# Moving a kernel's one odd-sized step from the last place to the last but one

## The chip, the cores and the metric

One core of one Trainium2 chip. The metric is device time in microseconds for one execution; a profiled run also gives the span from the first to the last instruction, some 2 us less.

In the profile's lines PE is TensorE (matmuls), PEld its loads of weights, DVE VectorE, ACT ScalarE, POOL GpSimd, which here also issues loads, and L443 is a line of the kernel. A line of a timeline has start and duration in us, engine, line, operation, output <- inputs, how many are merged (x4), and in brackets how long the engine stood idle before it and what ended that.

## The reference

The input x is 8 batches of 4224 tokens with 192 channels; t and s below index tokens.

```
x  = causal 7-tap convolution of the input, softmax taps per head (8 heads of 24 channels)
th = x @ w_theta
y  = w_tok_r @ (x * cos(th)) + w_tok_i @ (x * sin(th))       # over the 4224 tokens
u  = x + y
out = u + relu(u @ w_ch)
```

Nearly all the work is the two 4224 x 4224 token matmuls over 8 x 192 = 1536 columns.

## The kernel before

4224 tokens are 33 **row blocks** of 128 output tokens and 33 **chunks** of 128 input tokens. A chunk is prepared (convolution, transposes, theta, sine, products, sums) into seven fp16 operands `z`; up to 11 chunks are held at a time. A **step** visits a unit of row blocks with the active chunks. Sixteen units are pairs, done with seven products per chunk; unit 16 is the **single** block 32, with four. Each chunk meets all 17 units in 17 consecutive steps.

```python
    NU = (NT + 1) // 2                      # 17 units, NT = 33 row blocks
    ...
    base = [0, 0, 1, 1, 2, 3, 3, 4, 4, 5, 5]
    ...
    start = [base[k % NW] + (NU + 1) * (k // NW) for k in range(NK)]
    NSTEP = start[-1] + NU                  # 58
    shift = (NU - 1 - (NSTEP - 1)) % NU     # the single in step 57 (and 6, 23, 40)
    ...
    def unit(t):
        return (t + shift) % NU
```

Partial sums go to device memory between visits. x has to be added to each row block once. Where it can, GpSimd adds it to a block while it is loaded ("adds"); for the last five steps, which are short, an accumulating transfer adds it to the stored partial block beforehand ("ahead"), at a step worked out from the step's number:

```python
        self.late = self.final and self.n < NW
        ...
                if not self.late:
                    self.adds.append(i)
                else:
                    far = known <= start[2 * NW - 1]
                    self.ahead.append((i, 2 * NU - NW + 2 * (t % NU) if far else start[-1],
                                       (t // NU - 1 - far) % 2))
```

Work that is not a token matmul is placed among those of a step by position, in sevenths of the step. The positions that matter here:

```python
        for j, (r, i, which) in enumerate(here):        # additions "ahead"
            found.append((1.5 + 1.8 * j, lambda ...: r.add_ahead(i, which)))
        ...
            found.append((1.3 + 3 * (m - 1), lambda m=m: nxt.load_w(m)))    # weights for t + 2
        ...
                found.append((4.5, lambda k=k: load_chunk(k)))    # x of chunks that start at t + 2
        ...
                pos = [0, .5, 1.4, 2.2, 2.6, 3.1, 3.15, 3.4, 3.6]   # preparing a chunk for t + 1
```

The weights' loads and the additions are pinned in order on GpSimd's queue; the loads of x (`xw`, four per chunk) are not, and the framework's scheduler places them.

Of the kernel before, what the change touches and what calls it, by code (L numbers as in the profile page):

```python
# [16 lines left out]
def kernel(  # L17
# [42 lines left out]
    NU = (NT + 1) // 2  # L60
# [4 lines left out]
    assert len(base) == NW  # L65
    start = [base[k % NW] + (NU + 1) * (k // NW) for k in range(NK)]
    NSTEP = start[-1] + NU
    shift = (NU - 1 - (NSTEP - 1)) % NU

    NOSYNC = mybir.DependencyInfo(  # L70
        mybir.DependencyClass.NoSync, mybir.DependencyReason.DATA
# [664 lines left out]
```

## Time and profile before

Median 1449.51 us in the runs that the prediction had. The prediction shows the lines of the profile and what its steps take (y: token matmuls). Beside these, steps 0 to 3, which prepare the first chunks, take 86 us.

To read the steps: a step's y is known from the code, at 0.325 us per run of two matmuls (an unbroken stretch of the trace before has 104 in 16.90 us). What a step lasts beyond its y is the other work of TensorE plus its waits, and a comparison of such excesses, step by step, finds a lost microsecond in 58 steps.

### The profile page before, as it was taken

Reading aid. Unit: us, or ns where it says so; the run is one execution under the profiler, and the core shown is the slowest. Engines: PE = TensorE matmul, PEld = TensorE weight load, DVE = VectorE, ACT = ScalarE, POOL = GpSimd, SP = SyncE. Lnnn points to the kernel's source line nnn. Section 1 sums busy time; section 2 is a strip of 40 time slices with the busy share of each in tenths; the row PEclk is TensorE's granted clock in tenths of the full one; section 3 lists DMA queues with packets and bytes.
Section 4 is the critical chain, followed back from the end, with each engine's and each line's share of the span. In section 5 each row is a group of like instructions: output and inputs, shape, how many; then the busy total and the mean of one; then the engine's idle time right before and its main releaser. Section 6 shows DMA issues by size and latency. Waiting matters only on the chain.

```text
span 1446.4 us, 23748 instructions
## 1 busy us (share of the span) xinstructions
PE 1416.3 (98%) x9809; PEld 887.9 (61%) x9809; DVE 979.2 (68%) x1051; ACT 315.5 (22%) x379; POOL 435.1 (30%) x655
## 2 busy tenths in 40 slices
PE   7899999999999999999999999999999999999997
PEld 5556666666666666666666666666666666666665
DVE  6893555545548777866666657877777667767686
ACT  5861101111134254000000004435210110010133
POOL 7431211111233232432433342233323123213120
PEclk9999999999999999999999999999999999999999
DMA  9986756465699998998899989999999999998893
GB/s 173 227 178 145 146 103 149 90 149 97 137 231 219 214 250 217 228 254 183 213 256 213 242 143 245 228 188 234 279 216 206 209 204 221 204 203 194 166 222 125
DMA packets 272029, 281.99 MB, mean 195 GB/s; under 512 B 106672, under 2 KB 240176, under 8 KB 271920
## 3 DMA queue, kind: packets, MB, share of 16 engines
q0 software_dynamic: 162464, 92.15, 48.4%
q1 hardware_dynamic: 71824, 178.88, 35.1%
q10 hardware_dynamic: 37632, 9.44, 4.1%
q8 instruction: 77, 1.26, 0.3%
q14 instruction: 32, 0.26, 0.1%
HBM read 245.49 MB, written 108.13 MB: 244 GB/s over the span
## 4 chain that ended last, share of the span: by engine, by line
PE 89%; DVE 4%; DMA 3%; POOL 2%; ACT 1%; issue 1%; SPq 0%; DVEq 0%; ACTq 0%; POOLq 0%
PE y L443 82%; PE v L141 5%; PE pc L210 1%; PE tp L165 1%; POOL st L323 1%; DMA xw<-in_x_dram 1%; DVE z L257 1%; DVE wt L336 1%; DVE pv L408 1%; ACT z L246 1%; DVE z L251 0%; DVE pv L476 0%; DVE wt L348 0%; POOL xw L197 0%; DMA xs<-z 0%
## 5 line engine op out<-in xcount | busy, mean ns | idle before, releaser
L443 PE MATMUL y<-z,wt 128*128 128x384 f16 x7656 | 1283.6, 326 | 10.6 <-DVE pv L408 7.5
L443 PEld LDWEIGHTS <-wt 128*128 128x128 f16 x7656 | 740.8, 98 | 488.6 <-issue 10.6
L408 DVE TENSOR_TENSOR pv<-y,pv 128x768 f32<-128x768 f32 x324 | 308.9, 954 | 323.6 <-PE y L443 282.8
L336 DVE STREAM_TRANSPOSE wt<-st 128x1408 f16<-128x1408 f16 (+7 forms) x224 | 327.8, 1465 | 48.5 <-PE y L443 39.0
L323 POOL DMA_DIRECT2D st<-in_moe_w_tok_r_dram x232 | 132.5, 578 | 466.1 <-DVE wt L336 461.0
L323 POOL DMA_DIRECT2D st<-in_moe_w_tok_i_dram x232 | 132.7, 578 | 404.4 <-DVE wt L336 388.9
L348 DVE TENSOR_TENSOR wt<-wt 128x1408 f16<-128x1408 f16 (+7 forms) x216 | 176.7, 818 | 40.8 <-PE y L443 38.4
L151 ACT ACTIVATE z<-pc 128x768 f16<-128x768 f32 x65 | 53.2, 819 | 387.2 <-PE pc L210 386.9
L151 ACT ACTIVATE ub<-pv 128x768 f16<-128x768 f32 x63 | 50.2, 835 | 333.0 <-DVE pv L408 310.4
L406 ACT ACTIVATE pv<-y 128x768 f32<-128x768 f32 x66 | 54.0, 819 | 282.0 <-PE y L443 282.0
L141 PEld LDWEIGHTS <-uT 128*128 128x128 f16 x1056 | 91.0, 98 | 25.8 <-issue 7.9
L386 POOL TENSOR_TENSOR pv<-pv,xr 128x1536 f32<-128x1536 f32 x24 | 74.5, 3105 | 68.6 <-DVE pv L476 22.1
L197 POOL DMA_DIRECT2D xw<-in_x_dram x132 | 76.4, 585 | 31.0 <-DMA xw<-xw 8.7
L476 DVE SCALAR_TENSOR_TENSOR pv<-v,pv 128x768 f32<-128x768 f32 x66 | 62.9, 954 | 27.5 <-PE v L141 27.1
L257 DVE TENSOR_TENSOR z<-z 128x768 f16<-128x768 f16 x132 | 73.4, 556 | 3.6
L151 ACT ACTIVATE uT<-tp 128x1536 f16<-128x1536 f16 (+1 forms) x48 | 58.2, 1215 | 74.4 <-PE tp L165 74.4
L246 ACT ACTIVATE z<-v,half_pi 128x768 f16<-128x768 f32 x66 | 59.8, 907 | 41.2 <-PE v L141 40.8
L251 DVE TENSOR_TENSOR z<-z 128x1536 f16<-128x1536 f16 x66 | 60.0, 947 | 7.5 <-ACT z L246 7.5
L141 PE MATMUL v<-wth,uT 128*128 128x192 f16 x528 | 55.0, 248 | 4.4 <-ACT z L246 3.0
L141 PE MATMUL v<-wch,uT 128*128 128x192 f16 x528 | 54.2, 246 | 2.1 <-DVE pv L476 1.2
L246 ACT ACTIVATE z<-v 128x768 f16<-128x768 f32 x66 | 53.4, 809 | 0.0
L210 PE MATMUL pc<-xw,bands 96*64 96x192 f16 x528 | 35.8, 258 | 2.6 <-ACT bands L625 1.1
(44 smaller groups left out, 142.4 us busy)
## 6 DMA issues: line engine op xcount, KB each, us to landing
part<-pv SPq DMA_DIRECT2D x79, 768.0 KB, 4.3
pv<-part SPq DMA_DIRECT2D x79, 768.0 KB, 6.1
out_dram<-pv SPq DMA_DIRECT2D x66, 384.0 KB, 4.3
st<-in_moe_w_tok_r_dram POOLq DMA_DIRECT2D x136, 176.0 KB, 5.5
st<-in_moe_w_tok_i_dram POOLq DMA_DIRECT2D x136, 176.0 KB, 5.1
xs<-z SPq DMA_DIRECT2D x132, 96.0 KB, 4.5
xw<-in_x_dram POOLq DMA_DIRECT2D x121, 96.0 KB, 6.1
xr<-xs SPq DMA_DIRECT2D x24, 384.0 KB, 3.7
```

What stands on the lines that cost most here:

```text
L141: pe(nc.tensor.matmul(v[:, k, b * D : (b + 1) * D], lhsT=tT[:, 3 * k + b + i, :], rhs=w[:, 2 * b + i, :], start=(i == 0), stop=(i == 1),))
L151: act(nc.scalar.activation(out=out, in_=in_, func=AT.Copy))
L197: nc.gpsimd.dma_start(out=self.xw[lo : lo + n, h, :, :], in_=x[:, t0 : t0 + n, :].rearrange("b s d -> s b d"),)
L246: act(nc.scalar.activation(**args))
L257: dve(nc.vector.tensor_tensor(out=z[:, o, :], in0=z[:, a, :], in1=z[:, b, :], op=ALU.subtract))
L323: pool(nc.gpsimd.dma_start(out=st[a * Q : (a + 1) * Q, 0:nb, :, 0:n] .rearrange("i r bt s -> i (r bt) s"), in_=w[self.tbs[0] * P : (self.t ...
L336: dve(nc.vector.transpose(self.w[name][:, 0 : self.n, :, :], self.st[int(name[1])][:, int(name[0]) - 1, :, 0 : self.n * Q] .rearrange("p b ...
L348: dve(nc.vector.tensor_tensor(out=self.w[name][:, 0 : self.n, :, :], in0=self.w[a][:, 0 : self.n, :, :], in1=self.w[b][:, 0 : self.n, :, : ...
L386: ins = pool(nc.gpsimd.tensor_tensor(out=self.pv[i], in0=self.pv[i], in1=self.xr[i], op=ALU.add))
L408: dve(nc.vector.tensor_tensor(out=o, in0=yv, in1=o, op=ALU.add))
L443: pe(nc.tensor.matmul(y[cn][:, q, 0:BH], lhsT=self.w[wn][:, c, :, :].rearrange("p bt i -> p (bt i)"), rhs=chunks[k].z[:, zn, q * BH : (q + ...
L476: dve(nc.vector.scalar_tensor_tensor(out=ub, in0=channel_mix(self.uT[i][:, 6 * g : 6 * g + 6, :], wch), scalar=0.0, in1=ub, op0=ALU.max, o ...
```

## The change

Its intent is a better end: the single, the cheapest visit, is taken one step earlier, and the last step, when only two chunks are left, is a pair. One constant rotates the whole order of units.

```diff
-    shift = (NU - 1 - (NSTEP - 1)) % NU
+    shift = (NU - 1 - (NSTEP - 2)) % NU
```

The single moves from steps 6, 23, 40, 57 to 5, 22, 39, 56; all units, and the row blocks with them, move one step earlier.

## The prediction

> **What bounds the kernel now.** I read the page's engine table first, then the chain of waits, then cut TensorE's timeline into the kernel's 58 steps.
>
> ```profile
> PE 1416.3 (98%) x9809; PEld 887.9 (61%) x9809; DVE 979.2 (68%) x1051; ACT 315.5 (22%) x379; POOL 435.1 (30%) x655
> ...
> PE 89%; DVE 4%; DMA 3%; POOL 2%; ACT 1%; issue 1%; SPq 0%; DVEq 0%; ACTq 0%; POOLq 0%
> PE y L443 82%; PE v L141 5%; PE pc L210 1%; PE tp L165 1%; POOL st L323 1%; DMA xw<-in_x_dram 1%; DVE z L257 1%; DVE wt L336 1%; DVE pv L408 1%; ACT z L246 1%; DVE z L251 0%; DVE pv L476 0%; DVE wt L348 0%; POOL xw L197 0%; DMA xs<-z 0%
> ...
> L443 PE MATMUL y<-z,wt 128*128 128x384 f16 x7656 | 1283.6, 326 | 10.6 <-DVE pv L408 7.5
> ```
>
> The reader is to see that TensorE is busy 98% of the span and that token-mixing matmuls (y) alone carry 82% of the chain. Their 326 ns mean is an overlapped duration: 7656 of them lie in 1283.6 us of busy time, and the chain's unbroken stretches have 104 in 16.90 us, 0.1625 us each. One run of a weight against a chunk is two of them, 0.325 us.
>
> The code gives the length of every step: a pair of row blocks costs 7 runs per active chunk, the single block 4. Counting y matmuls along TensorE's timeline places each step. In most steps the time is y plus the other matmuls, with no gap: a pair with 11 chunks takes 25.0 us (y 25.04), one that also prepares two chunks and has 9 takes 26.7 (y 20.49, 6.2 of preparation). Two places differ: the single step that also prepares two new chunks (step 40), and the tail. The windows of steps 39, 40, 56, 57 and of what follows the last y matmul:
>
> ```profile
> core 0: us, PE busy (x) PEld busy (x) DVE busy (x) ACT busy (x) POOL busy (x), PEclk, DMA share, GB/s
> 975.20:1001.90 26.70, 26.70 (x216) 17.20 (x214) 17.46 (x23) 12.33 (x14) 9.17 (x16) 1.00 1.12 228
> 1001.90:1021.50 19.60, 18.51 (x163) 11.70 (x161) 17.43 (x20) 12.22 (x14) 4.04 (x8) 1.00 0.98 296
> 1412.40:1427.00 14.60, 13.74 (x114) 9.36 (x112) 10.34 (x13) 6.21 (x8) 0.00 (x0) 1.00 0.26 83
> 1427.00:1431.40 4.40, 4.12 (x32) 2.50 (x30) 3.93 (x6) 1.54 (x2) 0.00 (x0) 1.00 0.26 89
> 1431.40:1446.40 15.00, 6.89 (x78) 5.42 (x75) 7.31 (x9) 5.41 (x7) 0.00 (x0) 0.96 0.47 159
> ```
>
> Step 39 has TensorE full; step 40, 7 us shorter, does not. The last 15 us have every engine under half busy. There a cycle of cast, transpose, evacuation, channel matmul and final add runs, as the timeline's last lines show:
>
> ```profile
> 1430.77 1.82 DVE L408 TENSOR_TENSOR pv<-y,pv 128x768 f32<-128x768 f32 x2 [0.43 <-PE y L443]
> ...
> 1438.32 0.96 DVE L476 SCALAR_TENSOR_TENSOR pv<-v,pv 128x768 f32<-128x768 f32 x1 [0.98 <-PE v L141]
> 1438.60 0.34 PEld L165 LDWEIGHTS <-ub 128*128 128x128 f16 x6 [0.62 <-ACT ub L151]
> ...
> 1439.15 0.81 ACT L151 ACTIVATE uT<-tp 128x768 f16<-128x768 f16 x1 [0.60 <-PE tp L165]
> ...
> 1440.19 1.82 DVE L476 SCALAR_TENSOR_TENSOR pv<-v,pv 128x768 f32<-128x768 f32 x2 [0.91 <-PE v L141]
> ```
>
> VectorE adds the last token-mix sums at 1432.6 and finishes the last output at 1442.0, 9.4 us later; 4.4 us more go to the last store and the end.
>
> [...]
>
> **The change, part by part.** One constant rotates the order of the row blocks. Nothing is removed. Each chunk still meets all 17 units once, so y stays at 7656 matmuls, and counting from the code gives the same 79 partial stores, 79 loads, 24 additions of x and 9 early additions. The single moves from steps 6, 23, 40, 57 to 5, 22, 39, 56.
>
> *Start, steps 5 to 7: 0.* The four start-up steps with gaps (extras of 15.9, 14.2, 11.4 and 3.9 us over y) come before step 5 and keep their chunks. The single with 11 chunks took 14.30 us, all y, and will do so one step earlier.
>
> *Middle.* Before, of three inner singles only step 40 prepares two chunks while it runs. After, step 22 and step 39 both do, each with 9 chunks; step 40 becomes an ordinary pair. Step 40 took 19.58 us: y 11.71, so 7.87 of other time against 6.19 in step 39. Being squeezed costs 7.87 - 6.19 = **1.7 us**. Two squeezes in place of one: **+1.7**. Step 41 also loses 0.5 to what VectorE is left with (25.50 against 25.04); this too occurs about twice in place of once, **+0.4**.
>
> *Last steps.* Before: step 56, pair with 4 chunks, 28 runs; step 57, single with 2, 8 runs. After: single with 4, 16 runs; pair with 2, 14 runs. Six runs leave the end, 6 x 0.325 = 1.95 us; these lie in earlier steps, where TensorE is full, so step 56 begins **+1.95** later. What follows must be shorter by that to break even.
>
> From the start of step 56 to the last token add, the trace has 1412.4 to 1432.6 = **20.2 us**. After, VectorE limits this stretch. In step 56 TensorE has 5.2 us of y and about 4 of the previous step's transposes and outputs; VectorE has leftovers of step 55 (1.8), 3 additions of 0.95, 3 outputs of 0.96, and the next pair's weights: 4 transposes of 0.43 and 4 sums of about 0.25 (estimated from 0.41 for twice the size). That is about 10.3 us. In step 57 y is 14 x 0.325 = 4.55 us but there are 7 additions. Back to back each takes 0.91 (1.82 for two), so 6.4; with one more output 0.96 and a cast 0.55, about 7.9. TensorE must wait for each addition before it writes the same of its two sum buffers again. The sum is **18.2 us**, 2.0 less than before.
>
> After the last addition: still six output halves, but now two row blocks complete together. I walked the order of the code with the trace's durations (cast 0.55 or 0.84, transposes 0.5, evacuation 0.81, channel matmuls 0.82, final add 0.96, 0.1 for a hand-over). The two halves of the single are ready at once; the four of the pair share ScalarE (four evacuations, two casts: 4.9 us) and the two buffers of transposes and channel results. The last final add ends at about **10.0 us**, against 9.4 before: **+0.6**. Store and end: 4.4 in both.
>
> Sum: 1.7 + 0.4 + 1.95 - 2.0 + 0.6 = **+2.65 us**. To this I add 0.6 for the chance of the transfer wait below.
>
> **Rivals.** (1) *A transfer wait in step 39.* Its 26.7 us become about 19.6, while it loads x for the last two chunks, weights for two steps on and two partial blocks in place of one. The DMA share was already 1.12 there. The code lets the chunks' loads start in the middle of the step, and their median landing in this stretch is 8.0 us. Had they to wait, TensorE's first convolution of step 40 would stop for 2 to 6 us: 1455 to 1458. Against it: step 40 before moved 296 GB/s at a share of 0.98 with little loss. I give it one in five. (2) *A shorter tail.* If the outputs after the end overlap better than my walk, or step 57's additions hide beside TensorE, the last stretch gains 3 to 4 us and the total is a tie, 1448 to 1450. For it: VectorE has more work before the end in the new order and so less is left idle. Against it: two blocks end at once and only one engine evacuates. (3) *VectorE bounds the last steps harder.* If the seven additions alternate with TensorE rather than overlap, each round costs 0.95 + 0.65 + 0.1 for some of them, adding 2 to 3 us: 1455.
>
> **Range and chances.** 1449.5 + 2.65 + 0.6 = **1452.8 us**. The terms are uncertain by some 2 us each at the tail and up to 6 in step 39, so **1449.0 to 1457.0**. Two per cent is 29 us, the whole length of the tail; no term comes near. Faster by over 2%: 0.005; within: 0.985; slower: 0.01. The direction is less sure than the verdict: slower than before at about 85%.
>
> **What would show it.** y matmuls 7656 as before. Steps 22 and 39 about 19.6 us with 1 to 2 us of gaps, step 40 about 26.7 (longer with a wait of the convolution for x: rival 1). Step 56 starting 3.5 to 4.5 us later than 1412.4. VectorE nearly unbroken through steps 56 and 57, TensorE's y waiting on additions there. The last final add about 10 us after the last addition. The prediction is wrong if a transfer stalls TensorE in steps 22 to 24 or 38 to 41, or the tail changes by more than 3 us.

That a run keeps its price in another step, on which the +1.95 rests, was the assumption; in the result the 7656 y matmuls took 1283.2 us against 1283.6.

## The result, and the profile after

The changed kernel took **1457.72 us** (median of 4, 1454.78 to 1458.70) against 1449.14 (1448.48 to 1449.61). The ratio is 1.0056, 95% interval 1.0039 to 1.0074: slower by 0.6%, and within 2%. It was outside the predicted range by 0.7 us. (A ratio is the mean time of one kernel's runs over that of the other's of the same rounds, so not quite the ratio of the medians.)

The profiled run was the fastest of the four: span 1452.7 us against 1446.4. Its page's engine table, the head of its chain of waits, and the convolution's group:

```profile
PE 1415.5 (97%) x9809; PEld 886.8 (61%) x9809; DVE 976.8 (67%) x1051; ACT 315.2 (22%) x379; POOL 434.3 (30%) x655
...
PE 86%; DMA 6%; DVE 5%; ACT 2%; issue 1%; POOL 1%; SPq 0%; DVEq 0%; POOLq 0%; ACTq 0%
...
L210 PE MATMUL pc<-xw,bands 96*64 96x192 f16 x528 | 35.5, 255 | 6.0 <-DMA xw<-in_x_dram 3.7
```

TensorE's work is the same (1415.5 against 1416.3 us), but DMA's share of the chain rose from 3% to 6%, and the convolution now waits for the load of x, a releaser that its row of before did not name.

Excess over y by step, in the two profiled runs (of steps 0 to 55, those not listed agree within 0.2 us; 56 and 57 are taken together with the end, below):

| step | before: runs, excess | after: runs, excess |
|---|---|---|
| 22 | 63, 6.19 | 36 (single), **7.86** |
| 23 | 44 (single), 0.00 | 77, 0.46 |
| 36 | 63, 6.26 | 63, **9.02** |
| 39 | 63, 6.19 | 36 (single), **7.86** |
| 40 | 36 (single), 7.87 | 63, 6.59 |
| 41 | 77, 0.46 | 77, 0.00 |

Step 56 starts at 1413.63 us before and at 1420.31 after: 6.68 later. Six runs of y that now lie earlier are 1.95 of it, steps 22, 23, 39, 40 and 41 together 2.04, and **step 36 alone 2.76**. From there to the end it is 32.77 before and 32.39 after.

Step 36 is neither a single nor beside one. Windows of steps 35 and 36, first the kernel before, then after (columns as in the prediction's windows):

```profile
868.40:895.00 26.60, 26.60 (x215) 17.18 (x214) 20.57 (x25) 12.33 (x14) 9.12 (x16) 1.00 0.95 219
895.00:921.80 26.80, 26.80 (x217) 17.27 (x215) 22.46 (x28) 12.33 (x14) 6.87 (x12) 1.00 1.04 235
```

```profile
873.00:899.70 26.70, 26.70 (x216) 17.21 (x214) 21.27 (x26) 12.32 (x14) 11.59 (x19) 1.00 1.06 256
899.70:929.20 29.50, 26.98 (x216) 17.31 (x214) 22.38 (x28) 12.32 (x14) 7.87 (x14) 1.00 1.10 249
```

TensorE is idle for 2.5 us of step 36 after, and in step 35 GpSimd issues 19 instructions in place of 16. The timeline of GpSimd's issues and of the convolution shows which. Before:

```profile
875.80 2.29 POOL L323 DMA_DIRECT2D st<-in_moe_w_tok_r_dram  x4 [12.48 <-DVE wt L336]
878.08 2.29 POOL L197 DMA_DIRECT2D xw<-in_x_dram  x4
...
890.38 2.29 POOL L323 DMA_DIRECT2D st<-in_moe_w_tok_i_dram  x4 [10.02 <-DVE wt L336]
892.65 2.29 POOL L197 DMA_DIRECT2D xw<-in_x_dram  x4
```

After:

```profile
879.80 2.28 POOL L323 DMA_DIRECT2D st<-in_moe_w_tok_r_dram  x4 [12.49 <-DVE wt L336]
882.07 3.46 POOL L395 DMA_DIRECT2D part<-xs  x4
...
886.94 1.22 POOL L197 DMA_DIRECT2D xw<-in_x_dram  x2 [1.42 <-DMA st<-in_moe_w_tok_r_dram]
...
894.38 2.27 POOL L323 DMA_DIRECT2D st<-in_moe_w_tok_i_dram  x4 [6.21 <-DVE wt L336]
...
896.64 2.27 POOL L197 DMA_DIRECT2D xw<-in_x_dram  x4
...
902.91 0.52 PE L210 MATMUL pc<-xw,bands 96*64 96x192 f16 x7 [2.52 <-DMA xw<-in_x_dram]
```

Before, the four loads of the first chunk leave directly after the weights. After, four accumulating transfers (`part<-xs`, 384 KB each) stand there; they landed 10.0 us after their issue (median), where two stores of 768 KB in the same step took 5.1. Only two of the chunk's loads follow them, 13.9 us into the step (886.9 less its start at 873.0) where before's four left at 9.1 (878.1 less 869.0); the other two come behind the second weights (`st<-in_moe_w_tok_i_dram`), whose issue waits for VectorE to free a buffer (6.21 us). They leave at 896.6 and 897.2, and step 36 wants them at 900.1. They land 6.0 and 5.7 us after their issue, sooner than the 8.1 to 8.7 us that the four took before: they came late because they left late, not because they moved slowly.

Why they are there: the step of an early addition is 2 x 17 - 11 + 2 x (t mod 17). For the last step, t = 57, it is 35. Before, the last step was block 32, whose tokens come too late for that and are added in step 41; the others came out as 27, 29, 31 and 41. With blocks 0 and 1 last, the formula applies and gives 35, in which two chunks are prepared and two are loaded. The number of early additions, nine, is unchanged; their place is not.

### The profile page after: what moved, and what is told of

The parts are those of the page before. It is cut to its first block, busy times and chain, and to the rows that moved or that the text cites. A ratio compares the mean times of both kernels' runs of the same rounds, so it can differ in the third digit from the quotient of the medians.

```text
span 1452.7 us, 23747 instructions
## 1 busy us (share of the span) xinstructions
PE 1415.5 (97%) x9809; PEld 886.8 (61%) x9809; DVE 976.8 (67%) x1051; ACT 315.2 (22%) x379; POOL 434.3 (30%) x655
## 4 chain that ended last, share of the span: by engine, by line
PE 86%; DMA 6%; DVE 5%; ACT 2%; issue 1%; POOL 1%; SPq 0%; DVEq 0%; POOLq 0%; ACTq 0%
PE y L443 78%; PE v L141 5%; DMA st<-in_moe_w_tok_r_dram 1%; DMA xw<-in_x_dram 1%; PE pc L210 1%; PE tp L165 1%; DVE pv L408 1%; DMA xs<-z 1%; DVE wt L336 1%; ACT z L246 1%; DMA xw<-xw 1%; DVE z L257 1%; DVE z L251 1%; POOL st L323 1%; DMA pv<-part 1%
## 5 line engine op out<-in xcount | busy, mean ns | idle before, releaser
L443 PE MATMUL y<-z,wt 128*128 128x384 f16 x7656 | 1283.2, 326 | 12.8 <-DVE pv L408 9.7
L348 DVE TENSOR_TENSOR wt<-wt 128x1408 f16<-128x1408 f16 (+7 forms) x216 | 173.4, 803 | 43.4 <-PE y L443 41.1
```

The costliest lines, as they stand in the source:

```text
L348: dve(nc.vector.tensor_tensor(out=self.w[name][:, 0 : self.n, :, :], in0=self.w[a][:, 0 : self.n, :, :], in1=self.w[b][:, 0 : self.n, :, : ...
L443: pe(nc.tensor.matmul(y[cn][:, q, 0:BH], lhsT=self.w[wn][:, c, :, :].rearrange("p bt i -> p (bt i)"), rhs=chunks[k].z[:, zn, q * BH : (q + ...
```

## The experiments

**Theory.** The change costs what the prediction said of squeezed singles and of the end, and beyond that a wait for x in step 36 that comes from where the additions of blocks 0 and 1 are issued. **Rival one:** the wait belongs to the position of the single. **Rival two:** it is the additions' bytes, not their place in the queue. Four kernels ran first, on one chip, 5 rounds, with the kernel before at a median of 1449.91 us (1446.70 to 1453.93, 11 runs).

**r1, the changed kernel again.**

> The changed kernel once more, beside the others on the same chip. In its first profile step 36 lost 2.8 us to a convolution waiting for x, yet the profiled run (1454.8 us) was the fastest of four (up to 1458.7), so some 3.5 us more vary from run to run. Theory: the wait in step 36 is longer in other runs, expected median 1455 to 1459 with a spread of 2 to 4 us. Rival: the spread is chance of the chip that day, then before's runs here spread as much.

Median 1457.34 us (1456.72 to 1459.32), ratio 1.0057. As expected. Its spread is not beyond that of before in these rounds, so the rival about the spread is not excluded; but its profiled run, 1457.37 us, shows what a slower execution does. Step 36 lost 5.92 us (12.18 over y against 6.26). Windows around its wait (the last three columns: granted clock, DMA share, GB/s):

```profile
899.00:902.00 3.00, 0.81 (x5) 0.26 (x3) 2.97 (x4) 0.00 (x0) 2.27 (x4) 0.96 1.43 198
902.00:906.00 4.00, 3.19 (x15) 1.69 (x16) 0.14 (x1) 0.81 (x1) 0.00 (x0) 0.50 1.18 371
906.00:910.00 4.00, 4.00 (x24) 1.97 (x22) 0.71 (x1) 0.81 (x1) 0.00 (x0) 0.68 1.07 301
```

TensorE waited 3.00 us, and then its clock was 0.50 and 0.68 for 8 us: the wait was paid about twice. In the first profile a wait of 2.52 us left the clock at 1.00 (over the next 8 us). Step 3 shows the same of one fixed wait. TensorE stands 2.46 us there in all eleven profiles. In five of them (before, after, r1, r5, r7) its clock is 1.00 over the next 3 us and the step has 3.94 us over y; in the other six it is 0.54 to 0.64 and the step has 5.62. So two profiles can differ by 1.7 us in a step that no edit touches, and it is safer to compare steps than spans. The length of the wait alone does not decide what the clock does next: it was lower after 1.98 us (r7: 0.63 over 4 us), 2.46 (step 3, six profiles) and 3.00 (r1), and 1.00 after 2.46 (step 3, five profiles), 2.52 (the first profile) and 3.53 (r4 below, over 898 to 906 us). What does decide it is not shown.

**r2, the additions in a quiet step.**

```diff
-                    self.ahead.append((i, 2 * NU - NW + 2 * (t % NU) if far else start[-1],
+                    self.ahead.append((i, min(2 * NU - NW + 2 * (t % NU), 33) if far else start[-1],
```

> The changed kernel with one edit: the early additions of x to row blocks 0 and 1 are issued in step 33 (a quiet step) in place of step 35 (which prepares two chunks and loads two more). Theory: these four accumulating transfers stand ahead of the chunk loads and are the cause of the 2.8 us wait in step 36, so steps 35 and 36 go back to 26.7 us each, the time is 1449.1 + 3.5 = 1452 to 1453 us, and the spread falls to below 1 us. Rival: the wait comes from the rotation itself (other weights and rows at that time), then step 36 keeps over 1.5 us of gap and the time stays at 1455 to 1458.

1453.48 us (1452.74 to 1454.48), ratio 1.0026; 0.5 above the expected band and with a spread of 1.7 us, not below 1. Step 36 is back to 6.26 over y, and GpSimd's queue has the order of before in steps 35 and 36:

```profile
881.75 2.28 POOL L323 DMA_DIRECT2D st<-in_moe_w_tok_r_dram  x4 [12.49 <-DVE wt L336]
884.01 2.28 POOL L197 DMA_DIRECT2D xw<-in_x_dram  x4
896.33 2.28 POOL L323 DMA_DIRECT2D st<-in_moe_w_tok_i_dram  x4 [10.03 <-DVE wt L336]
898.60 2.28 POOL L197 DMA_DIRECT2D xw<-in_x_dram  x4
```

So the additions' place costs 1457.34 - 1453.48 = 3.9 us in the medians. Steps 22, 23, 39, 40 keep 7.86, 0.47, 7.86, 6.59.

**r3, the position of the single without the move of blocks 0 and 1.**

```diff
-            self.tbs = [tb for tb in (2 * self.u, 2 * self.u + 1) if tb < NT]
+            v = self.u if self.u == NU - 1 else (self.u - 1) % (NU - 1)
+            self.tbs = [tb for tb in (2 * v, 2 * v + 1) if tb < NT]
```

> The changed kernel with the same positions of pair and single, but the row blocks renamed so that the last pair is blocks 30 and 31 as in the kernel before (step 56 the single, step 57 the pair 30, 31) and no early addition falls into step 35. Theory: only the squeezes (+1.7, +0.4) and the shift of 6 runs with the shorter tail (+1.95 - 0.4) remain: 1452 to 1453.5 us, step 36 without a gap. Rival (the position of the single causes the wait in step 36): 1455 to 1458 us.

1453.91 us (1451.21 to 1454.01), ratio 1.0024; the median is 0.4 above the band. Step 36: 6.25 over y, no gap. The single stands where the change put it, and the wait is gone: rival one falls. What is left, about 4 us over before, is the position's own cost.

**r4, the suspected cause put into the kernel before.**

```diff
-                    self.ahead.append((i, 2 * NU - NW + 2 * (t % NU) if far else start[-1],
+                    self.ahead.append((i, (35 if t == 55 else 2 * NU - NW + 2 * (t % NU)) if far else start[-1],
```

> The kernel before with one edit: the early additions of row blocks 28 and 29 are issued in step 35 in place of step 31. Theory: the suspected cause alone, put into the kernel before, brings its wait: step 36 gets 2 to 4 us of gap behind a load of x, the time is 1451.5 to 1458 us and spreads more. Rival: nothing happens (within 0.7 us of before), and the wait in the changed kernel needs the new rotation.

1455.35 us (1454.36 to 1456.92), ratio 1.0040. Step 36: 10.05 over y, and the convolution waits as in the changed kernel:

```profile
898.46 0.27 PE L210 MATMUL pc<-xw,bands 96*64 96x192 f16 x1
902.26 0.52 PE L210 MATMUL pc<-xw,bands 96*64 96x192 f16 x7 [3.53 <-DMA xw<-in_x_dram]
```

The cause alone, with every unit in its old place, brings the wait. Gap and time are as expected; the spread, 2.6 us, is not more than that of before in these rounds.

The next four ran on one chip with before at 1448.98 us (1447.72 to 1451.95, 9 runs); r5 had 3 rounds, the others 5.

**r5, the additions still in step 35 but behind the loads of x.**

```diff
-            found.append((1.5 + 1.8 * j, lambda r=r, ...
+            found.append(((4.8 if t == 35 else 1.5) + (0.9 if t == 35 else 1.8) * j, lambda r=r, ...
```

> The changed kernel with the four accumulating transfers of row blocks 0 and 1 still issued in step 35, but behind both chunks' loads of x in GpSimd's queue in place of ahead of them. Theory A (order in the issuing queue: the loads leave late because the additions stand before them): no wait in step 36, 6.2 to 6.6 us over y there, 1452.5 to 1454.5 us as with the additions in step 33. Theory B (the additions' bytes crowd out the loads wherever they are issued in this step): steps 36 and 37 together still lose over 1.5 us, 1455 to 1458 us.

1452.63 us (1451.02 to 1453.66), ratio 1.0020. Step 36 has 6.25 and step 37 3.99 over y, although the same bytes are issued in the same step:

```profile
881.22 2.29 POOL L197 DMA_DIRECT2D xw<-in_x_dram  x4
...
893.52 2.29 POOL L323 DMA_DIRECT2D st<-in_moe_w_tok_i_dram  x4 [10.02 <-DVE wt L336]
895.80 2.29 POOL L197 DMA_DIRECT2D xw<-in_x_dram  x4
898.08 3.46 POOL L395 DMA_DIRECT2D part<-xs  x4
```

Here the bytes move behind the loads; where they moved before them, in the changed kernel, the late loads were not slow once issued (above). Together this fells rival two: the place in the queue decides.

**r6, r7, r8: is the squeeze what the prediction took it for?** r6 turns the rotation further, so that no single prepares chunks (steps 8, 25, 42). One notch short of that, 7, 24, 41, reads x before it is written and was not run.

```diff
-    shift = (NU - 1 - (NSTEP - 2)) % NU
+    shift = (NU - 1 - (NSTEP + 1)) % NU
-  ... 2 * NU - NW + 2 * (t % NU) if far
+  ... min(2 * NU - NW + 2 * (t % NU), 34) if far
```

> Another rotation: the single at steps 8, 25 and 42, where no step prepares chunks, the last steps all pairs; early additions kept out of step 35. Theory (the squeeze is a property of a single that prepares two chunks): no step has the 7.86 us over y, and steps 17 to 22 and 35 to 40 have 6.2 (4.0 with one chunk) each with nothing left over in the next step: 2.1 us less than before, 4.3 us less than the kernel with the additions in step 33. Its last steps, pairs with 4 and 2 chunks, are longer: some 37.5 us from the start of step 56, against 32.8 before, with 1.95 us of y more in them. Sum: 1448.5 to 1451.5 us, about as before. Rival (some other loss follows the rotation): steps 35 to 41 have gaps again.

1457.65 us (1456.48 to 1458.54), ratio 1.0054: a miss. The 7.86 is gone from every step, as the theory says, but step 40 has 12.14 over y and step 41 has 1.40, and step 56 to the end took 38.8 (expected: 37.5). In step 40 two row blocks of step 41, blocks 30 and 31, get their x from GpSimd just while VectorE prepares chunks. In the kernel before these two had their x added ahead, so this too is a placement that the rotation moved. The second of the two:

```profile
1031.90 3.92 DVE L257 TENSOR_TENSOR z<-z 128x768 f16<-128x768 f16 x2
1035.75 0.95 DVE L408 TENSOR_TENSOR pv<-y,pv 128x768 f32<-128x768 f32 x1
```

Two subtractions that take 0.56 us each elsewhere (515 to 560 ns in all 132 of the kernel before) took 3.92 together, beside a GpSimd addition that ran from 1031.95 for 3.46 us. The addition of y behind them came late, and TensorE waited 3.74 us for it. The first GpSimd addition, at 1022.25, did the same: one subtraction took 3.34 us, and TensorE waited 1.88 us. The two waits are all of step 40's loss. The second subtraction ended at 1035.83, 0.42 us after GpSimd's addition. That GpSimd's additions held the subtractions up is read from these times alone; how they would do it is not shown.

r7 (on r2) and r8 (on the kernel before) spread a chunk's tasks further apart in single steps:

```diff
                 pos = [0, .5, 1.4, 2.2, 2.6, 3.1, 3.15, 3.4, 3.6]
+                if not s.pair:
+                    pos = [0, .6, 1.6, 2.6, 3.5, 3.9, 3.95, 4.1, 4.2]
```

> The kernel with the additions in step 33, and in single steps the tasks of a new chunk are placed further apart in the order of TensorE's work (0, .6, 1.6, 2.6, 3.5 and on, in place of 0, .5, 1.4, 2.2, 2.6). Theory (in a squeezed step TensorE waits for ScalarE because less y lies between the dependent stages): steps 22 and 39 fall from 7.86 to 6.2 to 7.0 us over y, 1.5 to 3.5 us off the time: 1450 to 1452 us. Rival (VectorE or the transfers are what is short in these 19.6 us): 7.86 stays within 0.3.

> The kernel before with the same wider spacing in single steps. Only step 40 prepares chunks in a single. If spacing is the cause: step 40 from 7.87 to 6.2 to 7.0 us over y and the time 1 to 2 us below before (1447.5 to 1449). If not: the same as before within 0.5 us.

r8: 1450.70 us (1447.89 to 1453.42), ratio 1.0003. Step 40 fell from 7.87 to 6.47, and step 41 rose from 0.46 to 2.14; the 1 to 2 us that the theory would have gained did not come. The wait at its new place:

```profile
1031.14 2.11 PE L443 MATMUL y<-z,wt 128*128 128x384 f16 x12 [1.99 <-DVE pv L408]
```

The squeeze moved into the next step, where an addition of VectorE stands behind the chunk's products and sums; it did not go away. Over both steps the loss stays: 8.33 us over y before, 8.61 here. So it shows as waits for ScalarE in step 40 (1.08 us in three waits, in the kernel before), but a wider spacing does not remove it. (This profile, of r8's slowest run, also lost 2.26 us in step 25 and 0.8 in step 23, where the edit moves no task; why is open.)

r7: 1458.96 us (1457.50 to 1461.84), ratio 1.0067, a miss of 7 us and more. Steps 22 and 39 fell to 6.47, as the theory has it, but step 23 rose from 0.47 to 3.81 (a wait of 1.98 us as in r8, then a clock of 0.63 over 4 us), and step 40 from 6.59 to 14.76. In step 39 the scheduler had put one of the four loads of a new chunk behind the second weights:

```profile
987.56 1.72 POOL L197 DMA_DIRECT2D xw<-in_x_dram  x3
...
997.40 2.29 POOL L323 DMA_DIRECT2D st<-in_moe_w_tok_i_dram  x4 [8.13 <-DVE wt L336]
999.68 2.85 POOL L197 DMA_DIRECT2D xw<-in_x_dram  x5
...
1005.89 0.85 PE L210 MATMUL pc<-xw,bands 96*64 96x192 f16 x7 [5.75 <-DMA xw<-in_x_dram]
```

This is the wait of step 36 again, in another step and with no early addition near it: three loads at once, the fourth 12 us after the first, and TensorE stands 5.75 us and then runs 4 us at a clock of 0.50. So the early additions are one way to bring it about, not the only one.

**r9, the same test as r6 without the collision.** The single in steps 10, 27, 44 (`NSTEP + 3` in the line of r6). Run alone, 5 rounds; before at 1449.29 us.

> A rotation with the single at steps 10, 27 and 44, and with no addition of x for step 41 or 42. The rotation with the single at 8, 25 and 42 lost 7 us in steps 40 and 41, where subtractions of VectorE that take 0.56 us took up to 3.34 us while GpSimd added x. Theory (that addition beside the chunk preparation is the cause, and the squeeze belongs to a single that prepares chunks): steps 17 to 23 and 35 to 41 have 6.2 (4.0 with one chunk) over y and no gap; the stretch from step 56 to the end takes 38 to 39 us as in that rotation, and the sum is 4.1 us less before step 56 and 6 us more after it: about 2 us over before, 1450 to 1452.5 us. Rival (a late single-free end or a rotation as such costs more): 1454 us and over.

1460.49 us (1454.97 to 1465.39), ratio 1.0080: a miss in the time, by more than 8 us. Its profiled run, 1454.97 us, was its fastest. In it steps 17 to 23 and 35 to 41 are as the theory has them: 6.2 to 6.6 over y with two chunks, 4.0 with one, nothing left over. But step 28, behind a single, has 4.41: its row block waits for the transfer and GpSimd addition of x (the addition's engine stood idle 8.75 us for the transfer, VectorE 6.11 us for the addition),

```profile
707.75 0.96 DVE L408 TENSOR_TENSOR pv<-y,pv 128x768 f32<-128x768 f32 x1 [6.11 <-POOL pv L386]
```

and TensorE stands 2.57 us for that, then runs at a clock of 0.62 over 4 us. Why this came is not shown: step 26 of r6 stands behind a single too, with the same two blocks, and lost nothing. Why its other runs are up to 10 us slower is open; none of them was traced. No version here beats the kernel before; r8 equals it.

## Why the prediction was wrong

By its own parts:

*Nothing removed, same counts.* True, and the place of the failure. The text counted "9 early additions" before and after and gave them no cost; it never looked up in which step the formula puts those of blocks 0 and 1. **The step that failed is "The change, part by part": the moved additions were sized at 0, and they measured 2.76 us in the first profile, 5.92 in that of r1, and 3.9 in the medians** (r1 less r2). What the runs showed in their place is a path that the prediction did not follow: in step 35 the additions push half of a chunk's loads behind the second weights in GpSimd's queue, and the convolution of step 36 waits 2.5 to 3.0 us for them. r2, r3 and r5 each take them out of the way in a different manner, r4 puts them in.

*Start, 0.* Right: up to step 21 the two differ by 0.1 us. *Middle, +1.7 and +0.4.* Right: 7.86 in steps 22 and 39, 6.59 in step 40; in sum 2.04 against 2.1. r6 and r9 show that it belongs to a single that prepares chunks; r8 shows that this spacing does not win it back.

*Last steps.* +1.95 is right. The stretch to the last addition was 18.4 us (predicted 18.2), from there to the last final add 9.5 (10.0), then 4.4 (4.4). That the first agrees so well is partly luck. The prediction had VectorE as the bound in both steps, 10.3 us for step 56 and 7.9 for step 57. Step 56 took 8.8 us, with TensorE busy for 8.3 of them and VectorE for 6.8; from step 57 to the last addition it was 9.6. The two errors cancel. VectorE was the bound in step 57, 8.42 busy of 8.60 us, with y waiting for its additions:

```profile
1429.10:1437.70 8.60, 6.49 (x47) 3.87 (x45) 8.42 (x10) 1.54 (x2) 0.00 (x0) 1.00 0.40 135
```

A second error sits in the base: the start of step 56 before was put at 1412.4, because matmuls at the edges of the pieces of timeline were counted twice; it is 1413.63. So the stretch before is 19.0 us and not 20.2, and the end saves 0.4 us in place of 1.4. That is 1.0 us too little in the sum.

*Sum.* Without the additions the terms as measured give 1.95 + 2.04 - 0.38 = 3.6 us, and r2 and r3 sit 3.6 and 4.0 over the median of before in their rounds, inside the predicted range.

*Rivals.* The first was of the right kind, TensorE's convolution waiting for x, but in step 40 because of a short step 39; that did not happen in the changed kernel (6.59 there). It was given one chance in five and 2 to 6 us, which is what the real one, in step 36, cost; the size agreed by chance, as it was worked out for another step. None of the prediction's signs of being wrong came: it named stalls in steps 22 to 24 and 38 to 41 only. The second and third did not occur. The verdict (within 2%) and the direction were right; the range was not, by 0.7 us.

## What to carry to other kernels

When an order is rotated, list every placement that is computed from the position (here a formula in t mod 17), and see which step it lands in now; equal counts say nothing. For the loads of x what mattered here was what stood ahead of them in GpSimd's queue: in the changed kernel two of them left behind an issue that had waited 6.21 us for VectorE. With the additions ahead of the loads in step 35, step 36 had 9.02 us over y, and 12.18 in r1; with the same additions in the same step behind them, 6.25 (r5). So put urgent loads before an instruction that waits like this one (r5 does it by moving the additions; pinning the loads themselves and issuing the additions from another engine were not tried). In this kernel, with TensorE 97 to 98% busy, a wait of 3.00 us cost its step 5.92 us, as the clock was 0.50 and 0.68 over the next 8 us (r1); one of 2.52 us cost 2.76, at a clock of 1.00 (first profile).
